# One scaling and one reciprocal for both halves of the heads, in a fused attention and two-layer feed-forward kernel

## The chip, the cores and the metric

The kernel runs on one core of a Trainium2 chip. The engines are TensorE (PE, matrix products; its weight loads are a row of their own, PEld), VectorE (DVE), ScalarE (ACT), GpSimdE (POOL) and SyncE (SP, which issues the transfers). The metric is the time of one execution on the device in microseconds.

## The reference

The reference computes attention of 8 heads over 4 batches (512 local positions with a window of 32 to each side, and 32 global ones), and two feed-forward layers behind it. What the change touches is the softmax of the local positions:

```
def sm(s):
    s = s - np.max(s, axis=-1, keepdims=True)
    e = np.exp(s)
    return e / (np.sum(e, axis=-1, keepdims=True) + 1e-09)
...
s_l = np.concatenate([s_lg, s_ll], axis=-1)      # scores of the local queries
a_l = sm(s_l)
out_l = np.matmul(a_l, np.concatenate([v_g, v_l], axis=2))
...
h = x @ w_in                                     # 2304 x 512 times 512 x 2048
g = np.where(h > 0.0, h, alpha * (np.exp(np.minimum(h, 0.0)) - 1.0))
y = g @ w_out
```

A gated layer (w_gate, w_val, a second w_out) follows.

## The kernel before, in words

**Attention units.** The local attention is cut into 16 units, u = 4 x batch + tile of 128 queries. A unit has two halves, par = 0 and 1: the even and the odd heads, four of each. It goes through these steps:

- `a_S` on TensorE: scores s, one tile of 4 x 128 columns in PSUM per half (L229 puts in the mask, L235 the products).
- `a_E`: VectorE finds the maxima of each half (L254) and multiplies them by −0.125 (L255) into one small tile mx; ScalarE then takes the exponentials, four instructions per half (L257), each with its column of mx as bias. Only the first eight units do it so; later units have another form (L248, L250), which returns ahead of these lines.
- `a_T`: TensorE transposes (L263, tile ptp), ScalarE copies out of PSUM (L265, tile ET).
- `a_PV` on TensorE: product with the values (L276), whose last column is the sum of the exponentials, into one tile o per half.
- `a_N` on VectorE, in all 16 units: add 1e-9 to the sums (L289), reciprocal (L290), multiply (L291) into the result x.

**Blocks.** The four units of a batch make the 512 tokens of one block of the first feed-forward layer. x is transposed (`a_X`, L299 to L301) into xT. A block has 16 hidden blocks j of 128 columns: `mm1` makes h(j) on TensorE (12 matmuls, L132); ScalarE (L121, L122) and VectorE (L123) form the activation; ScalarE rounds it (L139) and VectorE forms the rest by a subtraction (L140), which together are g(j); `mm2` multiplies g(j) by the second matrix into y (12 matmuls, L146, in two parts of six). The second matmul of each three needs the rest, and so L140. TensorE does h(j+1) ahead of y(j).

**Weight tasks.** The weights come as 64-bit numbers and are decoded on the chip. There are 16 tasks for the first layer, numbered 0 to 15: a load of 1 MB (L75), absolute values on ScalarE (L83, tile dx), four steps on bits on VectorE (L90, L91, L92, L93), a rounding cast on ScalarE (L96) and a subtraction on VectorE (L99) into a tile wA. The tiles raw and dx have few buffers, so L93 of one task frees the buffer for the load of a later one.

**Order.** Units 0 to 3 and tasks 0 to 2 stand in an order written by hand for VectorE and ScalarE (`tc.manual_schedule`, L411 on). TensorE's order is written by hand for the whole kernel. From the first block on, a scheduler of the language sets the order on VectorE, ScalarE and the queue of transfers; each engine then runs its instructions in the order in which they stand. Units 4 to 7 run inside block 0 (`att_slot`): for hidden blocks 4i to 4i+3, unit 4+i has its scores at the first, its transpositions between the two parts of y in the second, and its product with the values in the third. So unit 6 belongs to hidden blocks 8 to 11, and its transpositions stand in the middle of y(8).

Of the kernel before, what the change touches and what calls it, by code (L numbers as in the profile page):

```python
# [13 lines left out]
ALU = mybir.AluOpType  # L14
# [7 lines left out]
P = 128  # L22
# [4 lines left out]
SCALE = 0.125  # L27
# [15 lines left out]
def fused_kernel(ctx: ExitStack, tc: tile.TileContext, kq, vl, gkq, gv, w_in, w_out, w_gate, w_val, w_o2, rms_g, consts, out):  # L43
    nc = tc.nc
# [141 lines left out]
    with ExitStack() as ls:  # L186
# [52 lines left out]
        def a_E(u):  # L239
            ss = s_t.pop(u)  # L240
            mx = small.tile([P, 2, 4], F32, tag="st", name="mx")
            e = [ap_.tile([P, 4, P], F32, tag=f"E{par}", name="E") for par in range(2)]
            if u >= 8:
                T = u % 4
                mk_u = mask32[:, 0 if T == 0 else (2 if T == 3 else 1), :]
                for par in range(2):
                    for pr in range(4):
                        nc.vector.tensor_tensor_reduce(out=e[par][:, pr, :], in0=ss[par][:, pr, :], in1=mk_u, scale=-SCALE, scalar=3.0e38,  # L248
                                                       op0=ALU.add, op1=ALU.min, accum_out=mx[:, par, pr:pr + 1])
                        nc.scalar.activation(e[par][:, pr, :], e[par][:, pr, :], AF.Exp, bias=mx[:, par, pr:pr + 1], scale=-1.0)  # L250
                e_t[u] = e
                return
            for par in range(2):
                nc.vector.tensor_reduce(out=mx[:, par, :], in_=ss[par], axis=AX.X, op=ALU.max)  # L254
                nc.vector.tensor_scalar(out=mx[:, par, :], in0=mx[:, par, :], scalar1=-SCALE, scalar2=None, op0=ALU.mult)  # L255
                for pr in range(4):
                    nc.scalar.activation(e[par][:, pr, :], ss[par][:, pr, :], AF.Exp, bias=mx[:, par, pr:pr + 1], scale=SCALE)  # L257
            e_t[u] = e
# [21 lines left out]
        def a_N(u):  # L280
            b, T = u // 4, u % 4
            if T == 0:
                x_t[b] = moe.tile([P, 4, 512], F32, tag="x32", name="x")
            x = x_t[b][:, T, :].rearrange("p (a e d) -> p e a d", a=4, e=2)
            os_ = o_t.pop(u)
            st = small.tile([P, 2, 4, 2], F32, tag="st", name="st")
            for par in range(2):
                o = os_[par]
                nc.vector.tensor_scalar(out=st[:, par, :, 0:1], in0=o[:, :, 64:65], scalar1=1e-9, scalar2=None, op0=ALU.add)  # L289
                nc.vector.reciprocal(st[:, par, :, 1:2], st[:, par, :, 0:1])  # L290
                nc.vector.tensor_tensor(out=x[:, par], in0=o[:, :, 0:64], in1=st[:, par, :, 1:2].to_broadcast([P, 4, 64]), op=ALU.mult)  # L291

        def a_X(b, cs, xT, pools):

# [11 lines left out]
        def att_slot(b, j, part):  # L306

            u, jj = 4 * (b + 1) + j // 4, j % 4
            if jj == 0 and part == 0:
                a_S(u, ATT2)  # L310
                a_E(u)
                load_kq(u + 1)
            if jj == 1 and part == 1:
                a_T(u, 0, aps, "att")
                a_T(u, 1, aps, "att")
            if jj == 2 and part == 0:
                a_PV(u, ATT2)
                a_N(u)
                load_v(u + 1)
# [91 lines left out]
        with tc.manual_schedule(engines={mybir.EngineType.DVE, mybir.EngineType.Activation}):  # L411
# [11 lines left out]
            a_S(0, ATT2)  # L423
            w1_bits(0)
            a_E(0)
            a_S(1, HB)
            a_T(0, 0, yps, "y0")
            a_T(0, 1, yps, "y1")
            w1_hi(0)
            a_E(1)  # L430
            a_PV(0, Y2)
            w1_lo(0)
            a_N(0)
            w1_abs(1)
            a_S(2, ATT2)
# [3 lines left out]
            w1_bits(1)  # L439
            a_PV(1, Y2)  # L440
            a_N(1)
            a_S(3, HB)
            a_T(2, 0, yps, "y0")
# [651 lines left out]
```

## Time and profile before

| what | us |
|---|---|
| median of 3 runs (lowest, highest) | 898.16 (897.08, 898.88) |
| the profiled execution, its own time | 896.49 |
| its span in the trace | 894.4 |
| TensorE busy | 862.2 (96%) |
| VectorE busy | 593.3 (66%) |
| ScalarE busy | 477.8 (53%) |

The profile is of one execution. Its span is what the trace covers; its own time is 2.1 us more. Busy shares are over the whole span, in which the first 160 us, with the attention units, differ from the rest.

### The profile page before, as it was taken

Reading aid. Unit: us, or ns where it says so; the run is one execution under the profiler, and the core shown is the slowest. Engines: PE = TensorE matmul, PEld = TensorE weight load, DVE = VectorE, ACT = ScalarE, POOL = GpSimd, SP = SyncE. Lnnn points to the kernel's source line nnn. Section 1 sums busy time; section 2 is a strip of 40 time slices with the busy share of each in tenths; the row PEclk is TensorE's granted clock in tenths of the full one; section 3 lists DMA queues with packets and bytes.
Section 4 is the critical chain, followed back from the end, with each engine's and each line's share of the span. In section 5 each row is a group of like instructions: output and inputs, shape, how many; then the busy total and the mean of one; then the engine's idle time right before and its main releaser. Section 6 shows DMA issues by size and latency. Waiting matters only on the chain.

```text
span 894.4 us, 16208 instructions
## 1 busy us (share of the span) xinstructions
PE 862.2 (96%) x6588; PEld 736.3 (82%) x6588; DVE 593.3 (66%) x1079; ACT 477.8 (53%) x863; POOL 19.2 (2%) x22
## 2 busy tenths in 40 slices
PE   4779999999999999999999999999999999999997
PEld 3567877888888888677888899997999998899985
DVE  4899988787677763543489566884365776365642
ACT  4677665555565454433556646664455665355531
POOL 0000000000000000000110101000100000000000
PEclk9999999999999999999999999999999999999999
DMA  9785375976678642441405532233222242133201
GB/s 359 301 307 194 121 263 178 294 275 189 227 259 287 219 168 112 172 153 60 168 1 208 181 95 95 95 119 117 83 95 95 95 131 70 60 118 119 93 25 36
DMA packets 60370, 139.46 MB, mean 156 GB/s; under 512 B 4872, under 2 KB 30728, under 8 KB 57736
## 3 DMA queue, kind: packets, MB, share of 16 engines
q1 hardware_dynamic: 60296, 138.43, 44.8%
q8 instruction: 52, 0.85, 0.4%
q14 instruction: 22, 0.18, 0.1%
HBM read 115.35 MB, written 23.07 MB: 155 GB/s over the span
## 4 chain that ended last, share of the span: by engine, by line
PE 78%; DVE 10%; DMA 5%; ACT 4%; issue 2%; SPq 1%; POOL 0%; ACTq 0%
PE A L751 15%; PE y L146 15%; PE h L132 15%; PE o L757 15%; PE Q L751 11%; DMA kq<-in_kq 2%; DVE dx L93 1%; DVE dx L92 1%; PE s L235 1%; PE ptp L263 1%; PE o L276 1%; PE hg L687 1%; DMA raw<-in_moe_w_out 1%; DVE wA L99 1%; DVE dx L90 1%
## 5 line engine op out<-in xcount | busy, mean ns | idle before, releaser
L146 PE MATMUL y<-g,wA 128*128 128x512 f32 x768 | 198.0, 401 | 4.8 <-DVE g L140 4.1
L132 PE MATMUL h<-xT,wA 128*128 128x512 f32 x768 | 186.6, 392 | 1.8 <-DVE xT L301 1.8
L146 PEld LDWEIGHTS y<-g,wA 128*128 128x128 f32 x768 | 140.3, 189 | 40.5 <-DVE g L140 6.1
L132 PEld LDWEIGHTS h<-xT,wA 128*128 128x128 f32 x768 | 143.6, 188 | 32.7 <-DVE xT L301 2.4
L751 PE MATMUL A<-xc,wS 128*128 128x384 f32 (+1 forms) x864 | 156.0, 329 | 1.1 <-ACT t L958 0.6
L751 PEld LDWEIGHTS A<-xc,wS 128*128 128x128 f32 x864 | 145.0, 188 | 5.9 <-ACT t L958 0.9
L757 PE MATMUL o<-wB,p 128*128 128x512 f32 x612 | 147.4, 393 | 0.7 <-DVE p L762 0.3
L757 PEld LDWEIGHTS o<-wB,p 128*128 128x128 f32 x612 | 113.7, 188 | 24.6 <-DVE p L762 2.5
L751 PE MATMUL Q<-xc,wS 128*128 128x384 f32 (+1 forms) x648 | 115.3, 326 | 0.0
L751 PEld LDWEIGHTS Q<-xc,wS 128*128 128x128 f32 x648 | 107.8, 188 | 0.0
L607 DVE TENSOR_TENSOR wS<-wraw,wS 128x1024 fp32r<-128x1024 f32 x63 | 78.5, 1246 | 35.7 <-ACT wS L606 35.6
L766 DVE TENSOR_TENSOR t<-t,Q 128x384 f32<-128x384 f32 (+1 forms) x108 | 55.9, 528 | 36.6 <-PE Q L751 24.0
L606 ACT CAST wS<-wraw 128x1024 fp32r<-128x1024 f32 x63 | 65.9, 1050 | 18.5 <-PE Q L751 11.4
L121 ACT ACTIVATE e<-h 128x512 f32<-128x512 f32 x48 | 28.9, 602 | 78.8 <-PE h L132 78.7
L139 ACT CAST g<-e 128x512 fp32r<-128x512 f32 x64 | 39.7, 621 | 48.8 <-DVE e L123 32.2
L123 DVE SCALAR_TENSOR_TENSOR e<-e,h 128x512 f32<-128x512 f32 x48 | 32.6, 679 | 34.8 <-ACT e L122 34.8
L140 DVE TENSOR_TENSOR g<-e,g 128x512 fp32r<-128x512 f32 x64 | 43.9, 686 | 10.1 <-ACT g L139 9.7
L762 DVE TENSOR_TENSOR p<-p,p 128x384 fp32r<-128x384 f32 x36 | 20.0, 557 | 43.1 <-ACT p L761 43.1
L83 ACT ACTIVATE dx<-raw 128x1024 f32<-128x1024 f32 x34 | 38.9, 1148 | 10.5 <-DMA raw<-in_moe_w_out 3.5
L92 DVE SCALAR_TENSOR_TENSOR dx<-raw,dx 128x1024 int32<-128x1024 int32 x34 | 42.1, 1245 | 0.8
L93 DVE SCALAR_TENSOR_TENSOR dx<-raw,dx 128x1024 int32<-128x1024 int32 x34 | 41.4, 1220 | 0.3
L761 ACT CAST p<-p 128x384 fp32r<-128x384 f32 x36 | 18.4, 514 | 41.6 <-PE o L757 41.5
(176 smaller groups left out, 872.1 us busy)
## 6 DMA issues: line engine op xcount, KB each, us to landing
wraw<-wS SPq DMA_DIRECT2D x63, 512.0 KB, 3.2
raw<-in_moe_w_out SPq DMA_DIRECT2D x14, 1024.0 KB, 7.6
raw<-in_moe_w_in SPq DMA_DIRECT2D x8, 1024.0 KB, 7.2
raw<-in_moe_w_gate SPq DMA_DIRECT2D x6, 1024.0 KB, 5.6
raw<-in_moe_w_val SPq DMA_DIRECT2D x6, 1024.0 KB, 6.4
wS<-raw SPq DMA_DIRECT2D x48, 128.0 KB, 2.3
gvr<-in_gv SPq DMA_DIRECT2D x8, 640.0 KB, 4.1
wS<-dx SPq DMA_DIRECT2D x36, 128.0 KB, 2.1
```

The source lines that it names most:

```text
L83: ins = nc.scalar.activation(x, f(words(raw)[:, :, 1]), AF.Abs)
L92: nc.vector.scalar_tensor_tensor(out=i32(x), in0=word[:, :, 1], scalar=-0x40000000, in1=i32(x), op0=ALU.bitwise_and, op1=ALU.bitwise_or)
L93: nc.vector.scalar_tensor_tensor(out=i32(x), in0=word[:, :, 0], scalar=29, in1=i32(x), op0=ALU.logical_shift_right, op1=ALU.bitwise_or)
L132: nc.tensor.matmul(h[:, :n], W1[c, G][:, ws, o:o + P], xT[c][:, xs, :n], start=(k == 0), stop=(k == 11))
L139: nc.scalar.copy(g[:, 0, :n], e[:, :n])
L140: nc.vector.tensor_tensor(out=g[:, 1, :n], in0=e[:, :n], in1=f(g[:, 0, :n]), op=ALU.subtract)
L146: nc.tensor.matmul(ys[dc][:, :n], W2[j][:, ws, dc * P:(dc + 1) * P], g[:, gs, :n], start=(j == 0 and k == 0), stop=(j == 15 and k == 2))
L606: nc.scalar.copy(t[:, :, 0, :], raw)
L607: nc.vector.tensor_tensor(out=t[:, :, 1, :], in0=raw, in1=f(t[:, :, 0, :]), op=ALU.subtract)
L751: nc.tensor.matmul(ps[:, :n], w[:, 2 * (q % 4) + c, ws, :], x[:, c, xs, :n], start=(first and c == 0 and z == 0), stop=(c == 1 and z == 2) ...
L757: nc.tensor.matmul(o, p[:, pp, t * P:(t + 1) * P], Wo[j][:, ww, :], start=(first and z == 0), stop=(last and z == 2))
L766: nc.vector.tensor_tensor(out=t, in0=t, in1=ps, op=ALU.add)
```

## The change

In `a_E` of the first eight units the scaling of the maxima is one operation on 8 columns behind both reduces, where it was one on 4 columns behind each. In `a_N` of all units the two additions come first, then one reciprocal of 8 columns, then the two multiplications. There are 24 VectorE instructions fewer (8 scalings, 16 reciprocals). The lines of the exponentials, the copies and the multiplications become L258, L266 and L292.

```
             for par in range(2):
                 nc.vector.tensor_reduce(out=mx[:, par, :], in_=ss[par], axis=AX.X, op=ALU.max)
-                nc.vector.tensor_scalar(out=mx[:, par, :], in0=mx[:, par, :], scalar1=-SCALE, scalar2=None, op0=ALU.mult)
+            nc.vector.tensor_scalar(out=mx, in0=mx, scalar1=-SCALE, scalar2=None, op0=ALU.mult)
+            for par in range(2):
                 for pr in range(4):
                     nc.scalar.activation(e[par][:, pr, :], ss[par][:, pr, :], AF.Exp, bias=mx[:, par, pr:pr + 1], scale=SCALE)
...
             for par in range(2):
-                o = os_[par]
-                nc.vector.tensor_scalar(out=st[:, par, :, 0:1], in0=o[:, :, 64:65], scalar1=1e-9, scalar2=None, op0=ALU.add)
-                nc.vector.reciprocal(st[:, par, :, 1:2], st[:, par, :, 0:1])
-                nc.vector.tensor_tensor(out=x[:, par], in0=o[:, :, 0:64], in1=st[:, par, :, 1:2].to_broadcast([P, 4, 64]), op=ALU.mult)
+                nc.vector.tensor_scalar(out=st[:, par, :, 0:1], in0=os_[par][:, :, 64:65], scalar1=1e-9, scalar2=None, op0=ALU.add)
+            nc.vector.reciprocal(st[:, :, :, 1:2], st[:, :, :, 0:1])
+            for par in range(2):
+                nc.vector.tensor_tensor(out=x[:, par], in0=os_[par][:, :, 0:64], in1=st[:, par, :, 1:2].to_broadcast([P, 4, 64]), op=ALU.mult)
```

TensorE's order is the same as before. The scheduler's order on VectorE and ScalarE changes between the first subtraction L140 and the end of block 0. Three places follow, before and with the change; numbers of tiles differ between the two programs.

ScalarE around the exponentials of unit 6, before. dx_1373 and wA_1379 are of weight task 12, g_1242 of hidden block 8, e_1340 of block 9, E_1288 and E_1289 the exponentials of unit 6:

```order
L83 ACTIVATE dx_1457<-raw_1180 128x1024
L139 CAST g_1242<-e_1238 128x512
L257 ACTIVATE E_1288<-s_1245,mx_1287 128x128 x4
L257 ACTIVATE E_1289<-s_1246,mx_1287 128x128 x4
L121 ACTIVATE e_1340<-h_1327 128x512
L122 ACTIVATE e_1340<-e_1340 128x512
L265 COPY ET_1358<-ptp_1353 128x512
L265 COPY ET_1365<-ptp_1360 128x512
L96 CAST wA_1379<-dx_1373 128x2x512
L139 CAST g_1344<-e_1340 128x512
```

The exponentials stand right behind the rounding of block 8, ahead of block 9's activation and of task 12's cast.

The same place with the change. wA_1366 is of task 12, dx_1484 of task 14, g_1230 of block 8, e_1327 of block 9, E_1276 and E_1277 are unit 6:

```order
L83 ACTIVATE dx_1443<-raw_1168 128x1024
L139 CAST g_1230<-e_1226 128x512
L121 ACTIVATE e_1327<-h_1314 128x512
L122 ACTIVATE e_1327<-e_1327 128x512
L96 CAST wA_1366<-dx_1360 128x2x512
L258 ACTIVATE E_1276<-s_1233,mx_1275 128x128 x4
L258 ACTIVATE E_1277<-s_1234,mx_1275 128x128 x4
L139 CAST g_1331<-e_1327 128x512
L266 COPY ET_1345<-ptp_1340 128x512
L83 ACTIVATE dx_1484<-raw_1211 128x1024
L266 COPY ET_1352<-ptp_1347 128x512
```

Block 9's activation and task 12's cast moved ahead of the exponentials, and task 14's absolute values between the two copies behind them.

VectorE from the subtraction of block 8 (g_1242) on, before; mx_1287 are unit 6's maxima:

```order
L255 TENSOR_SCALAR mx_1287<-mx_1287 128x4
L140 TENSOR_TENSOR g_1242<-e_1238,g_1242 128x512
L255 TENSOR_SCALAR mx_1287<-mx_1287 128x4
L91 TENSOR_SCALAR dx_1373<-dx_1373 128x1024
L91 TENSOR_SCALAR dx_1457<-dx_1457 128x1024
L92 SCALAR_TENSOR_TENSOR dx_1373<-raw_1094,dx_1373 128x1024
L92 SCALAR_TENSOR_TENSOR dx_1457<-raw_1180,dx_1457 128x1024
L93 SCALAR_TENSOR_TENSOR dx_1373<-raw_1094,dx_1373 128x1024
L123 SCALAR_TENSOR_TENSOR e_1340<-e_1340,h_1327 128x512
```

The scalings stand on both sides of the subtraction.

With the change, from the subtraction of block 8 (g_1230) on; dx_1360 is task 12, dx_1443 task 13:

```order
L140 TENSOR_TENSOR g_1230<-e_1226,g_1230 128x512
L93 SCALAR_TENSOR_TENSOR dx_1360<-raw_1083,dx_1360 128x1024
L255 TENSOR_SCALAR mx_1275<-mx_1275 128x8
L91 TENSOR_SCALAR dx_1443<-dx_1443 128x1024
L123 SCALAR_TENSOR_TENSOR e_1327<-e_1327,h_1314 128x512
L92 SCALAR_TENSOR_TENSOR dx_1443<-raw_1168,dx_1443 128x1024
L99 TENSOR_TENSOR wA_1366<-dx_1360,wA_1366 128x2x512
L93 SCALAR_TENSOR_TENSOR dx_1443<-raw_1168,dx_1443 128x1024
L140 TENSOR_TENSOR g_1331<-e_1327,g_1331 128x512
```

The one scaling of unit 6 stands behind task 12's L93, which stands behind the subtraction; block 9's subtraction (g_1331) has one L91 and one L92 fewer ahead of it.

VectorE between the subtractions of blocks 9 (g_1344) and 10 (g_1399), before; st_1436 and o_1402 belong to unit 6, dx_1498 to task 14:

```order
L140 TENSOR_TENSOR g_1344<-e_1340,g_1344 128x512
L99 TENSOR_TENSOR wA_1463<-dx_1457,wA_1463 128x2x512
L289 TENSOR_SCALAR st_1436<-o_1402 128x4
L289 TENSOR_SCALAR st_1436<-o_1403 128x4
L123 SCALAR_TENSOR_TENSOR e_1395<-e_1395,h_1382 128x512
L290 RECIPROCAL st_1436<-st_1436 128x4 x2
L90 TENSOR_SCALAR dx_1498<-dx_1498 128x1024
L291 TENSOR_TENSOR x_861<-o_1402,st_1436 128x4x64
L291 TENSOR_TENSOR x_861<-o_1403,st_1436 128x4x64
L140 TENSOR_TENSOR g_1399<-e_1395,g_1399 128x512
```

With the change, up to the subtraction of block 10 (g_1386); ahead of these rows stand L90 and L91 of task 14 (dx_1484) behind block 9's subtraction, and dx_1583 is task 15:

```order
L99 TENSOR_TENSOR wA_1449<-dx_1443,wA_1449 128x2x512
L92 SCALAR_TENSOR_TENSOR dx_1484<-raw_1211,dx_1484 128x1024
L93 SCALAR_TENSOR_TENSOR dx_1484<-raw_1211,dx_1484 128x1024
L90 TENSOR_SCALAR dx_1583<-dx_1583 128x1024
L289 TENSOR_SCALAR st_1423<-o_1389 128x4
L123 SCALAR_TENSOR_TENSOR e_1382<-e_1382,h_1369 128x512
L289 TENSOR_SCALAR st_1423<-o_1390 128x4
L91 TENSOR_SCALAR dx_1583<-dx_1583 128x1024
L290 RECIPROCAL st_1423<-st_1423 128x8
L99 TENSOR_TENSOR wA_1490<-dx_1484,wA_1490 128x2x512
L92 SCALAR_TENSOR_TENSOR dx_1583<-raw_1312,dx_1583 128x1024
L140 TENSOR_TENSOR g_1386<-e_1382,g_1386 128x512
```

Task 14 whole, and half of task 15, moved ahead of block 10's subtraction. In the queue of transfers one pair changes places: the values of unit 7 now stand behind the first weights of the gated layer.

## Rows read from the trace of the kernel before

**Rows 1.** Busy us of each engine by stretch; then clock, transfers' share, GB/s.

```profile
60.00:80.00 20.00, 18.70 (x147) 14.74 (x147) 20.00 (x32) 12.46 (x18) 0.00 (x0) 1.00 0.77 286
160.00:300.00 140.00, 140.00 (x1293) 114.25 (x1292) 106.88 (x236) 74.79 (x138) 0.00 (x0) 1.00 0.76 255
```

**Rows 2.** Timeline of VectorE, unit 0's maxima: start, duration, engine, instruction.

```profile
14.35 0.68 DVE L254 TENSOR_REDUCE mx<-s 128x4 f32<-128x512 f32 x1
15.07 0.17 DVE L255 TENSOR_SCALAR mx<-mx 128x4 f32<-128x4 f32 x1
15.15 0.69 DVE L254 TENSOR_REDUCE mx<-s 128x4 f32<-128x512 f32 x1
```

**Rows 3.** Timeline of VectorE, a stretch without gaps, for steps between starts.

```profile
120.77 1.22 DVE L93 SCALAR_TENSOR_TENSOR dx<-raw,dx 128x1024 int32<-128x1024 int32 x1
121.90 0.69 DVE L91 TENSOR_SCALAR dx<-dx 128x1024 int32<-128x1024 int32 x1
122.50 0.68 DVE L123 SCALAR_TENSOR_TENSOR e<-e,h 128x512 f32<-128x512 f32 x1
123.10 1.22 DVE L92 SCALAR_TENSOR_TENSOR dx<-raw,dx 128x1024 int32<-128x1024 int32 x1
124.24 1.22 DVE L99 TENSOR_TENSOR wA<-dx,wA 128x1024 fp32r<-128x1024 f32 x1
```

**Rows 4.** Timeline of VectorE, unit 0's normalization, first half and start of the second.

```profile
20.78 0.15 DVE L289 TENSOR_SCALAR st<-o 128x4 f32<-128x4 f32 x1
20.97 0.18 DVE L290 RECIPROCAL st<-st 128x4 f32<-128x4 f32 x1
21.18 0.42 DVE L291 TENSOR_TENSOR x<-o,st 128x256 f32<-128x256 f32 x1
21.52 0.15 DVE L289 TENSOR_SCALAR st<-o 128x4 f32<-128x4 f32 x1
```

**Rows 5.** Timeline of three engines at the start; idle time before, and its releaser, in brackets.

```profile
19.64 1.23 DVE L99 TENSOR_TENSOR wA<-dx,wA 128x1024 fp32r<-128x1024 f32 x1 [2.01 <-ACT wA L96]
...
30.28 2.17 ACT L257 ACTIVATE E<-s,mx 128x128 f32<-128x128 f32 x8 [1.62 <-DVE mx L255]
...
33.92 1.15 PE L276 MATMUL o<-v,ET 128*32 128x65 f32 x64 [1.04 <-ACT ET L265]
...
36.29 1.64 PE L299 MATMUL xtp<-ident,x 128*128 128x128 f32 x13 [0.74 <-DVE x L291]
```

**Rows 6.** Timeline of VectorE and TensorE in hidden blocks 1 and 2.

```profile
55.89 0.69 DVE L90 TENSOR_SCALAR dx<-dx 128x1024 f32<-128x1024 f32 x1 [0.64 <-ACT dx L83]
...
66.49 2.79 PE L146 MATMUL y<-g,wA 128*128 128x512 f32 x11 [1.30 <-DVE g L140]
```

**Rows 7.** Timeline of VectorE, ScalarE and TensorE around hidden block 8 and unit 6.

```profile
104.51 0.69 DVE L140 TENSOR_TENSOR g<-e,g 128x512 fp32r<-128x512 f32 x1
...
104.70 2.17 ACT L257 ACTIVATE E<-s,mx 128x128 f32<-128x128 f32 x8 [0.39 <-DVE mx L255]
...
109.91 1.05 ACT L96 CAST wA<-dx 128x1024 fp32r<-128x1024 f32 x1 [0.93 <-DVE dx L93]
...
105.37 1.53 PE L146 MATMUL y<-g,wA 128*128 128x512 f32 x6
...
107.54 1.62 PE L146 MATMUL y<-g,wA 128*128 128x512 f32 x6
```

**Rows 8.** Timeline of the queue of transfers, ScalarE and TensorE, tasks 14 and block 10.

```profile
109.95 2.09 SPq L75 DMA_DIRECT2D raw<-in_moe_w_out  x2
...
114.87 1.12 ACT L83 ACTIVATE dx<-raw 128x1024 f32<-128x1024 f32 x1 [1.02 <-DMA raw<-in_moe_w_out]
...
118.73 2.88 PE L146 MATMUL y<-g,wA 128*128 128x512 f32 x12
```

**Rows 9.** TensorE behind its longest wait: busy by stretch with clock, and the timeline.

```profile
48.00:54.00 6.00, 3.69 (x14) 3.10 (x15) 5.96 (x10) 5.54 (x14) 0.00 (x0) 0.72 1.01 401
...
50.31 2.50 PE L146 MATMUL y<-g,wA 128*128 128x512 f32 x5 [2.57 <-DVE g L140]
```

## The prediction

> **What bounds the kernel now.** I first read busy time by stretch of time. From 160 us on TensorE is busy in all of the time, so whatever it loses before then moves the end by as much [rows 1]. Between 60 and 80 us VectorE is busy without a gap and TensorE is not: there VectorE's order of work decides when TensorE gets its next operand [rows 1]. That stretch holds the scheduled units 4 to 7, where the weight tasks, the hidden blocks and the attention units share VectorE. So a saving on VectorE can be worth something, and a change in its order can cost as much. The profiled execution took 896.49 us, 1.67 below the median of the three runs shown, 898.16; I make the sum against the profiled execution and add the result to the median.
>
> **The single operations.** In the first units each half took 0.72 us from the reduce to its dependent scaling and 0.08 us from there to the next reduce, 1.60 us for both halves [rows 2]. The trace has no two adjacent reduces followed by one scaling, nor an operation on eight elements. Independent operations of about 0.68 us start 0.60 us after each other [rows 3], so I take 0.60 + 0.72 + 0.08 = 1.40: 0.20 us less per unit on VectorE. Its bound is 0 below (a wider operation as dear as two) and 0.24 above (with the removed scaling its own 0.17 and the step behind it, at most). But the first half's exponentials now wait for the second half's reduce, 0.60 us more. The normalization took 0.19 + 0.21 + 0.34 per half, 1.48 us [rows 4]; merged it is 0.07 + 0.19 + 0.21 + 0.34 + 0.34 = 1.15, or 0.33 less, once both halves of the output are there. I take four elements more in an operation as free: the 0.17 us of 4 elements against 0.68 us of 512 leaves about 1 ns an element [rows 2].
>
> **The start (units 0 to 3, order written by hand).** The 0.60 us goes down ScalarE's queue, through the exponentials of unit 0 to the cast that VectorE's subtraction at 19.64 waited 2.01 us for [rows 5]; that subtraction moves to 20.24. Behind it the savings work it off: unit 0's normalization saves 0.33, unit 2's scaling 0.20, unit 1's normalization 0.33, so VectorE reaches unit 3's reduces 0.26 to 0.35 us sooner. The 0.60 us wait of unit 3's own exponentials takes that back: they start at about 30.5 instead of 30.28 [rows 5]. The product with the values follows them, from 33.92 to 34.15, ends at 35.30 instead of 35.07, and only then can the merged reciprocal of unit 3 start: 35.35 + 0.19 + 0.21 + 0.34 + 0.43 is 36.5, where the transpositions went on at 36.29 [rows 5]. **Start: +0.3 us**, bounded by −0.3 (all the wait hidden) and +0.6 (none).
>
> **VectorE's order up to hidden block 8.** The scheduler changed it: the difference of the two orders, counted from the subtraction of block 0 to that of block 8 (L140), is three scalings and two reciprocals fewer, but one L91 and one L92 more ahead of it. By the steps between starts [rows 3], 0.60 + 1.14, that is 1.74 less 5 x 0.07 to 0.08: +1.4 us. Against it stands an idle 0.64 us, in which VectorE waited for task 5's absolute values [rows 6]; they now come ahead of two copies on ScalarE, and VectorE reaches them later, so that gap closes. **Net +0.8 us**, between +0.4 and +1.4. With the start, block 8's subtraction moves from 104.51 to about 105.6 [rows 7].
>
> **The wait at unit 6.** Before, ScalarE ran unit 6's eight exponentials from 104.70, ahead of everything of block 9, and TensorE went through the transpositions without a wait into the second half of y(8) at 107.54 [rows 7]. Now block 8's subtraction is followed on VectorE by task 12's L93 and only then by the scaling, and on ScalarE by task 12's cast, which needs that L93, ahead of the exponentials. From the subtraction's start: 0.60, then L93 1.22 [rows 3], the cast 1.05, the exponentials 2.17, and about 0.15 for the last transposition [rows 7]. That is 5.2 us, so y(8)'s second half starts at 105.6 + 5.2 = 110.8. It was 3.03 behind the subtraction. **+3.2 us in all at this point**, of which 2.1 is the new wait. Queued behind the exponentials are block 9's cast and the copies that unit 6's product with the values needs; TensorE comes to them late as well.
>
> The Trainium skill, "PSUM — Partial Sum Buffer", Engine vs sequencer instructions, states that ScalarE's, VectorE's and GpSimdE's queues are strict first in, first out, which speaks against this change: by it the exponentials cannot pass the cast. By it the sum below stands; without it the exponentials could start with their maxima, the 2.1 us would go and 900.9 us would come out. The trace agrees where it can: VectorE stood 2.01 us behind a cast with other work queued [rows 5].
>
> **The wait at hidden block 10.** Between the subtractions of blocks 9 and 10 VectorE had one L90 and one L99 of the weight tasks before; now two L90, two L91, two L92, one L93 and two L99 stand there. Block 9's subtraction comes at 105.6 + 0.60 + 1.13 + 0.07 + 0.60 + 0.60 + 1.14 + 1.13 + 1.13 = 112.0. Then VectorE wants task 14, whose load took 4.9 us from issue at 109.95 to 114.87 [rows 8]; its buffer is now free at 105.6 + 1.8, so it lands near 112.4 and ScalarE has it done at 113.5. Task 13's cast stands behind that and a copy of half its size: 113.5 + 0.55 + 1.05 = 115.1. From there VectorE does L99, L92, L93, L90, two L289, L123, L91, the reciprocal, L99, L92: 4 x 1.14 + 1.26 + 3 x 0.60 + 3 x 0.07, near 7.9 us (1.26 is an L92 whose successor needs it, 0.12 more, as from a reduce to its scaling [rows 2]), and block 10's subtraction starts at 123.0, done at 123.8. TensorE reaches y(10) by 110.8 + (118.73 − 107.54) = 122.0 at the latest [rows 7, 8], and its second matmul needs that operand at 122.2. It waits 1.6 us or a little more. Before, that matmul ran at 118.96; now at 123.85. **+4.9 us in all at this point.** What hid the subtraction before was that it stood ahead of tasks 14 and 15; 0 to 2.4 us of wait are the bounds, by an earlier and a later landing of task 14.
>
> **The sum.** 0.3 + 0.8 + 2.1 + 1.7 = 4.9. After block 10 VectorE has idle time again and TensorE sets the pace, so nothing gives it back [rows 1]. The other edits cost nothing that ends last: in units 8 to 15 only reciprocals merge, beside a TensorE that never waits; if that cover were gone they would save 0.08 us each. In profiled time 896.49 + 4.9 = 901.4; on the median **898.16 + 4.9, about 903.0 us**.
>
> **Rivals.**
> *The saving comes through (faster).* Four units x (0.20 + 0.33), four x 0.15 for two operations fewer, eight x 0.08: 3.3 us, time 894.9. For it: VectorE full from 60 to 80 us [rows 1]. It decides if L93 and the cast of task 12 finish before TensorE needs unit 6, which takes VectorE 2 us ahead of my sums. Chance 0.08.
> *One wait only.* Unit 6 waits, block 10 does not, because task 14 lands earlier or TensorE comes later: +3.2 us, 901.4. Chance 0.15.
> *The clock falls as well.* After a wait of 2.57 us TensorE's five matmuls took 2.50 us, against six in 1.53 later, with a granted clock of 0.72 over that stretch, that is between its two levels of 1.2 and 2.4 GHz; after 1.30 us it did not fall (11 matmuls in 2.79) [rows 6, 7, 9]. The new waits, about 1.4 us with half-busy transpositions behind it and 1.6 to 2.1 us, lie between these. A fall costs about 1.2 us each: 904.2 to 905.5. Chance 0.25.
> *No change.* The lateness is absorbed: VectorE's order is as good as the old one, and my sums of it are too long by the 3 us or so that the two waits need. Against it speaks that the cast stands ahead of the exponentials whatever the times are. Within 0.2%, near 898.2. Chance 0.12.
>
> **How the numbers follow.** My forecast, both waits at an unchanged clock, has 0.40 and its own range 901.9 to 904.0. The range for all, 899.0 to 906.0, leaves out the faster case and most of no change. Beyond 0.2%, 1.8 us, a measurement of this kernel tells a time from no change. Slower: 0.40 + 0.25 + 0.15 = 0.80; same 0.12; faster 0.08.
>
> **What would show it.** The profile after should have a wait of transpositions for exponentials between 107 and 111 us, a wait of y for L140 near 122 us, full busy time behind 160 us, the reciprocal once per unit, and the transpositions of the first block going on at 36.6 instead of 36.29. I am wrong if unit 6's exponentials start by 106, if block 8's subtraction stands before 105 us, or if waits of over 1 us appear or go in the stretch 145 to 155 us, which I take as unchanged.

## The result, and the profile after

The changed kernel took 903.51 us (median of 6 runs, 902.13 to 905.26) against 898.45 us for the kernel before (6 runs, 897.08 to 899.21): the ratio is 1.0063, with a 95% interval of 1.0052 to 1.0073. In a second set of runs it was 1.0071 (1.0055 to 1.0087). The change makes the kernel slower by 5 to 6 us; 903.0 was predicted.

The profiled execution of the changed kernel took 903.48 us, close to its median. That of the kernel before took 896.49 us, 1.96 us under the median of these six runs, so that the two traces differ by 7.0 us where the medians differ by 5.06. I read places from the traces and sizes from the medians.

The busy time by stretch answers to [rows 1]; columns are PE, PEld, DVE, ACT, POOL, granted clock, transfers' share, GB/s:

```profile
60.00:80.00 20.00, 19.10 (x208) 14.93 (x207) 20.00 (x28) 11.73 (x15) 0.00 (x0) 1.00 0.74 263
160.00:300.00 140.00, 140.00 (x1252) 114.13 (x1233) 105.17 (x240) 77.33 (x146) 0.00 (x0) 1.00 0.75 252
```

VectorE still has no gap between 60 and 80 us, and TensorE still has none from 160 to 300 us: what is lost before then stays lost. The merged operations on VectorE's timeline (units 0 and 1, maxima, then unit 0's normalization) answer to [rows 2, 4]:

```profile
14.10 1.28 DVE L254 TENSOR_REDUCE mx<-s 128x4 f32<-128x512 f32 x2
15.41 0.17 DVE L255 TENSOR_SCALAR mx<-mx 128x8 f32<-128x8 f32 x1
15.49 1.28 DVE L254 TENSOR_REDUCE mx<-s 128x4 f32<-128x512 f32 x2
...
21.13 0.23 DVE L289 TENSOR_SCALAR st<-o 128x4 f32<-128x4 f32 x2
21.39 0.20 DVE L290 RECIPROCAL st<-st 128x8 f32<-128x8 f32 x1
21.63 0.76 DVE L292 TENSOR_TENSOR x<-o,st 128x256 f32<-128x256 f32 x2
```

A unit's maxima take 15.49 − 14.10 = 1.39 us (before 1.60, predicted 1.40). Eight elements cost what four did, 0.17. So each single step came out as worked out, to 0.03 us, and the saving on VectorE's own time is real. The start, from the timelines of VectorE and TensorE, answers to [rows 5]:

```profile
19.99 1.23 DVE L99 TENSOR_TENSOR wA<-dx,wA 128x1024 fp32r<-128x1024 f32 x1 [3.01 <-ACT wA L96]
...
32.57 1.09 PE L277 MATMUL o<-v,ET 128*32 128x65 f32 x30 [2.40 <-issue]
...
33.59 1.97 PE L264 MATMUL ptp<-ident,E 128*128 128x128 f32 x8
...
38.22 1.64 PE L300 MATMUL xtp<-ident,x 128*128 128x128 f32 x13 [0.83 <-DVE x L292]
```

The transpositions go on at 38.22, 1.93 us later than before and not 0.3. The subtraction waits 3.01 us for the cast, where it waited 2.01. Two things on TensorE add to it: a gap of 2.40 us inside unit 2's product with the values (1.40 before, also put down to "issue": the profile shows nothing that was waited for), and a lower granted clock behind it. The same product and unit 3's transpositions in the kernel before:

```profile
31.20 0.66 PE L276 MATMUL o<-v,ET 128*32 128x65 f32 x30 [1.40 <-issue]
31.79 1.09 PE L263 MATMUL ptp<-ident,E 128*128 128x128 f32 x8
```

The clock by stretch, in the changed kernel:

```profile
30.00:34.00 4.00, 1.59 (x38) 1.26 (x33) 0.91 (x5) 3.11 (x9) 0.00 (x0) 0.77 1.04 429
34.00:38.00 4.00, 3.30 (x75) 2.47 (x73) 3.12 (x9) 2.33 (x3) 0.00 (x0) 0.81 0.99 372
```

The same two stretches of the kernel before:

```profile
30.00:34.00 4.00, 1.75 (x42) 1.42 (x45) 2.95 (x10) 3.72 (x11) 0.00 (x0) 1.00 1.04 430
34.00:38.00 4.00, 3.19 (x80) 2.62 (x80) 2.80 (x9) 2.85 (x5) 0.00 (x0) 1.00 1.02 378
```

The clock is 0.77 and 0.81 where it was 1.00, so for part of the time TensorE ran at the lower of its two levels. Hidden block 8 and unit 6, from the timelines of VectorE, ScalarE and TensorE, answer to [rows 7]:

```profile
107.56 0.69 DVE L140 TENSOR_TENSOR g<-e,g 128x512 fp32r<-128x512 f32 x1
108.16 1.22 DVE L93 SCALAR_TENSOR_TENSOR dx<-raw,dx 128x1024 int32<-128x1024 int32 x1
109.29 0.17 DVE L255 TENSOR_SCALAR mx<-mx 128x8 f32<-128x8 f32 x1
...
109.41 1.05 ACT L96 CAST wA<-dx 128x1024 fp32r<-128x1024 f32 x1
110.37 2.17 ACT L258 ACTIVATE E<-s,mx 128x128 f32<-128x128 f32 x8
...
111.56 0.66 PE L264 MATMUL ptp<-ident,E 128*128 128x128 f32 x4 [1.83 <-ACT E L258]
112.59 0.66 PE L264 MATMUL ptp<-ident,E 128*128 128x128 f32 x4 [0.38 <-ACT E L258]
113.00 1.64 PE L146 MATMUL y<-g,wA 128*128 128x512 f32 x6
```

The chain is the predicted one, link by link: subtraction, L93, cast, exponentials, transpositions. From the subtraction to the second half of y(8) it takes 113.00 − 107.56 = 5.44 us, predicted 5.2, before 3.03. The scaling itself was done at 109.46; the exponentials then stood behind the cast for 0.9 us although they lacked nothing. Hidden block 10, the same three engines:

```profile
115.49 0.70 DVE L90 TENSOR_SCALAR dx<-dx 128x1024 f32<-128x1024 f32 x1 [0.83 <-ACT dx L83]
...
124.87 0.69 DVE L140 TENSOR_TENSOR g<-e,g 128x512 fp32r<-128x512 f32 x1
...
123.90 0.39 PE L146 MATMUL y<-g,wA 128*128 128x512 f32 x1
125.61 2.79 PE L146 MATMUL y<-g,wA 128*128 128x512 f32 x11 [1.32 <-DVE g L140]
```

y(10)'s second matmul waits 1.32 us for the subtraction, at an unchanged clock (11 matmuls in 2.79). Before, it ran 6.65 us earlier. All waits of TensorE from 60 to 300 us, longest last in a row:

```profile
PE y L146 <- DVE g L140: 2.9, 3, 1.3
PE ptp L264 <- ACT E L258: 2.6, 3, 1.8
PE h L132 <- DVE xT L302: 0.5, 1, 0.5
```

In the kernel before these three were 1.3, 0.4 and 0.5 us. So the two predicted waits are there, and no third of over 1 us.

### The profile page after: what moved, and what is told of

The parts are those of the page before. It is cut to its first block, busy times and chain, and to the rows that moved or that the text cites. A ratio compares the mean times of both kernels' runs of the same rounds, so it can differ in the third digit from the quotient of the medians.

```text
span 901.6 us, 16174 instructions
## 1 busy us (share of the span) xinstructions
PE 864.9 (96%) x6588; PEld 736.5 (82%) x6588; DVE 591.2 (66%) x1055; ACT 478.8 (53%) x863; POOL 19.2 (2%) x22
## 4 chain that ended last, share of the span: by engine, by line
PE 82%; DVE 7%; DMA 5%; ACT 3%; issue 2%; SPq 0%; POOL 0%; ACTq 0%
PE y L146 17%; PE h L132 16%; PE A L752 15%; PE o L758 14%; PE Q L752 11%; DMA kq<-in_kq 2%; PE s L235 2%; PE o L277 1%; PE ptp L264 1%; DVE dx L92 1%; DMA raw<-in_moe_w_in 1%; PE hg L688 1%; DMA wraw<-wS 1%; PE go L860 1%; DVE dx L93 1%
## 5 line engine op out<-in xcount | busy, mean ns | idle before, releaser
L140 DVE TENSOR_TENSOR g<-e,g 128x512 fp32r<-128x512 f32 x64 | 44.0, 687 | 10.4 <-ACT g L139 10.0
L92 DVE SCALAR_TENSOR_TENSOR dx<-raw,dx 128x1024 int32<-128x1024 int32 x34 | 42.3, 1246 | 0.8
L93 DVE SCALAR_TENSOR_TENSOR dx<-raw,dx 128x1024 int32<-128x1024 int32 x34 | 41.6, 1223 | 0.3
```

What stands on the lines that cost most here:

```text
L92: nc.vector.scalar_tensor_tensor(out=i32(x), in0=word[:, :, 1], scalar=-0x40000000, in1=i32(x), op0=ALU.bitwise_and, op1=ALU.bitwise_or)
L93: nc.vector.scalar_tensor_tensor(out=i32(x), in0=word[:, :, 0], scalar=29, in1=i32(x), op0=ALU.logical_shift_right, op1=ALU.bitwise_or)
L140: nc.vector.tensor_tensor(out=g[:, 1, :n], in0=e[:, :n], in1=f(g[:, 0, :n]), op=ALU.subtract)
```

## The experiments

In block 0 an order can be imposed on VectorE and ScalarE instruction by instruction, with the work itself unchanged. That separates the two things that the change did at once: it merged operations, and it made the scheduler choose another order. To follow a loss or a gain through a run I took from each trace the starts of TensorE's product h and subtracted those of the kernel before. Each column is one start, named by its time before; each row is one profiled execution, in us:

| kernel | 39.22 | 55.37 | 83.21 | 108.99 | 121.45 | 149.45 | 175.45 | 480.27 |
|---|---|---|---|---|---|---|---|---|
| changed kernel | +1.9 | +2.3 | +2.9 | +5.5 | +6.8 | +6.1 | +6.1 | +5.8 |
| the same, again | +1.5 | +3.3 | +3.3 | +6.0 | +7.5 | +6.8 | +6.8 | +6.4 |
| start_only | +0.2 | +0.3 | +0.2 | +0.2 | +0.2 | −0.2 | −0.2 | −0.4 |
| merged_old_order | +1.7 | +3.5 | +3.6 | +3.9 | +3.6 | +4.0 | +4.0 | +3.7 |
| split_new_order | −0.2 | +0.2 | +0.8 | +3.6 | +5.2 | +4.7 | +4.7 | +4.4 |
| unit6_early | +2.1 | +2.5 | +3.1 | +3.7 | +10.7 | +10.1 | +10.0 | +9.8 |
| block10_early | +1.3 | +3.2 | +3.4 | +6.0 | +5.6 | +5.0 | +5.0 | +4.6 |
| both_early | +2.4 | +2.8 | +3.1 | +3.8 | +3.5 | +3.5 | +5.0 | +4.6 |
| order_split | +0.6 | −2.5 | −4.4 | −4.4 | −4.7 | −3.1 | +4.2 | +3.9 |
| order_merged | +0.7 | −2.7 | −5.0 | −4.5 | −4.9 | −3.8 | +2.7 | +2.3 |
| order_split_2 | +0.6 | −2.5 | −4.5 | −4.5 | −4.9 | −1.3 | +0.7 | +0.8 |
| order_merged_2 | +0.2 | −3.3 | −5.5 | −5.1 | −5.5 | −4.5 | −0.8 | −1.1 |
| order_merged_3 | +2.2 | −1.2 | −3.5 | −3.1 | −3.4 | −1.9 | −0.5 | +4.1 |

Differences to before by the medians are given below as the ratio's, times the median of before in the same set of runs, with the 95% interval in brackets.

### Order or merging: three kernels

**start_only** merges in units 0 to 3 alone (the edit is against the changed kernel; the later units keep the two steps of before):

```diff
-            nc.vector.tensor_scalar(out=mx, in0=mx, scalar1=-SCALE, scalar2=None, op0=ALU.mult)
+            if u < 4:
+                nc.vector.tensor_scalar(out=mx, in0=mx, scalar1=-SCALE, scalar2=None, op0=ALU.mult)
...
-            nc.vector.reciprocal(st[:, :, :, 1:2], st[:, :, :, 0:1])
+            if u < 4:
+                nc.vector.reciprocal(st[:, :, :, 1:2], st[:, :, :, 0:1])
```

> Both operations are merged in units 0 to 3 alone, the ones in the order written by hand; all other units stay split, and the order of block 0 is that of the kernel before. Order theory (the time is lost in the scheduler's new order of block 0): +0.3 us, about 898.7. Rival (the waiting for both halves at the start is what costs; in the changed kernel's profile the first transpositions went on 1.9 us later than before): +1.9 us, about 900.4.

Measured: 897.86 against 897.40, ratio 1.0003 (0.9993 to 1.0013), +0.3 us (−0.6 to +1.2). Its transpositions went on at 36.49. As the order theory had it; +1.9 lies outside the interval. So the merging at the start does not by itself cost the 1.93 us that the changed kernel's profile shows there.

**merged_old_order** is the whole change with the order of before in block 0 (the diff is in the order alone: one list per engine, each instruction tied behind the one ahead of it in the list):

```diff
+        in_order(<VectorE's instructions of block 0 as before, second scaling and second reciprocal only>)
+        in_order(<ScalarE's instructions of block 0 as before>)
```

> The whole change, but in block 0 VectorE and ScalarE run their instructions in the order of the kernel before (the merged scaling and reciprocal stand where the second of each pair stood). Order theory: nearly all of the loss goes, the start's +0.3 and the few tenths saved by the merging remain: 898.0 to 898.8. Rival (the merging itself costs, since each merged step waits for both halves): the loss stays, about 903.

Measured: 899.09 against 897.40, ratio 1.0015 (1.0001 to 1.0028), +1.3 us (0.1 to 2.5). The two waits are gone, and 903 is excluded; but it is 1 us dearer than I gave it. Its row in the table shows where: the start, and +1.8 between 39 and 55 us. There unit 4's one scaling stands behind an L99, since the second of the pair had stood there; its exponentials started at 53.16 (50.73 before, and 1.7 of the difference are the start), the transpositions waited 0.96 us for them, and the six matmuls behind ran in 2.91 us instead of 1.64, with a granted clock of 0.50 from 54 to 58 us. The changed kernel's order has the scaling behind the same L99, so this cost is not peculiar to the order of before: the second profile of the changed kernel (after_again, below), in the scheduler's order, loses 1.8 us there as well. First merged_old_order, then after_again:

```profile
54.35 2.14 PE L290 MATMUL ptp<-ident,E 128*128 128x128 f32 x8 [0.96 <-ACT E L284]
56.15 2.91 PE L167 MATMUL y<-g,wA 128*128 128x512 f32 x6
...
54.19 2.15 PE L264 MATMUL ptp<-ident,E 128*128 128x128 f32 x8 [0.79 <-ACT E L258]
55.98 2.91 PE L146 MATMUL y<-g,wA 128*128 128x512 f32 x6
```

In the first profile of the changed kernel the five matmuls ahead of the transpositions were slower (2.20 us, against 1.43 in merged_old_order), the wait was 0.20 and the loss 0.4. What this place costs differs between executions.

**split_new_order** merges nothing and takes the changed kernel's order:

```diff
-                nc.vector.tensor_scalar(out=mx, in0=mx, scalar1=-SCALE, ...)   # one for both halves
+                <one for each half, side by side>; reciprocals likewise
+        in_order(<VectorE's and ScalarE's instructions of block 0 as in the changed kernel>)
```

> Nothing is merged: the operations are those of the kernel before, but in block 0 VectorE and ScalarE run in the order of the changed kernel (the pairs of scalings and reciprocals side by side where the merged one stands). Order theory: +4.6 us, about 903. Rival (the merging itself costs): no change, about 898.5.

Measured: 902.29 against 897.40, ratio 1.0048 (1.0033 to 1.0063), +4.3 us (3.0 to 5.7). The order alone brings both waits, without a single merged operation. From TensorE's timeline:

```profile
109.67 0.66 PE L290 MATMUL ptp<-ident,E 128*128 128x128 f32 x4 [1.82 <-ACT E L279]
...
124.05 2.79 PE L167 MATMUL y<-g,wA 128*128 128x512 f32 x11 [1.65 <-DVE g L161]
```

1.82 and 1.65 us, against 1.83 and 1.32 in the changed kernel. In its trace ScalarE's queue and the queue of transfers have the changed kernel's order throughout. So 4.3 of the 5 to 6 us come with the scheduler's order alone. The whole merging in the order of before costs 1.3 us (0.1 to 2.5); in neither kernel of that order is it a saving that the medians show.

### Putting the order back in pieces: three kernels

**unit6_early**, on VectorE and on ScalarE:

```diff
 L140 of block 8
+L255 of unit 6
 L93 of task 12
-L255 of unit 6
...
+L258 of unit 6, x8
 L121, L122 of block 9
 L96 of task 12
-L258 of unit 6, x8
```

> The changed kernel with one edit of its order: unit 6's scaling goes ahead of task 12's L93, and its eight exponentials ahead of block 9's activation and task 12's cast, as before the change. The wait at unit 6 (1.8 us) should go. Theory (VectorE's order still lets block 10's subtraction start at 124.9 us, so TensorE only waits there longer, 3 us and more where it was 1.3): 902.9 to 903.5. Rival (the two waits simply add up): 1.8 to 2.1 us of the loss go, about 901.5.

Measured: 906.67 against 897.40, ratio 1.0097 (1.0079 to 1.0115), +8.7 us, 3 us more than the changed kernel. The rival is refuted, and my theory, which had no extra loss, missed as well. The wait of 1.83 us at unit 6 did go. From VectorE's, ScalarE's and TensorE's timelines:

```profile
111.97 0.69 DVE L144 SCALAR_TENSOR_TENSOR e<-e,h 128x512 f32<-128x512 f32 x1 [1.72 <-ACT e L143]
...
114.85 1.31 DVE L93 SCALAR_TENSOR_TENSOR dx<-raw,dx 128x1024 int32<-128x1024 int32 x1
...
121.42 1.13 ACT L83 ACTIVATE dx<-raw 128x1024 f32<-128x1024 f32 x1 [3.73 <-DMA raw<-in_moe_w_out]
...
125.20 0.50 PE L167 MATMUL y<-g,wA 128*128 128x512 f32 x1 [2.06 <-ACT g L160]
128.08 4.23 PE L167 MATMUL y<-g,wA 128*128 128x512 f32 x11 [2.38 <-DVE g L161]
```

Block 9's activation, now behind the exponentials, kept VectorE waiting for 1.72 us; task 13's L93 behind it started at 114.85 instead of 112.83; that L93 frees the buffer for task 15's load, so task 15's absolute values came at 121.42 instead of 118.91; and on ScalarE block 10's activation stood behind them. y(10) then waited twice, 2.06 and 2.38 us, and its 11 matmuls took 4.23 us, with a granted clock of 0.68 from 128 to 133 us, where they take 2.79 at 1.00. The wait had moved to the end of a chain through a transfer and grown.

**block10_early** takes the order of before from block 9's subtraction to the end of block 0, on VectorE and on ScalarE. The part on VectorE up to block 10's subtraction:

```diff
 L140 of block 9
-L90, L91 of task 14
 L99 of task 13
-L92, L93 of task 14, L90 of task 15
 L289 x2, L123 of block 10, L290 of unit 6
-L91 of task 15, L99 of task 14, L92 of task 15
+L90 of task 14, L292 x2
 L140 of block 10
```

> The changed kernel, but from hidden block 9's subtraction on VectorE and ScalarE have the order of the kernel before, so that block 10's subtraction stands ahead of tasks 14 and 15. Unit 6's wait is left as it is. Theory of two waits (each costs what it shows): the wait of y(10) for L140 goes, that of unit 6's transpositions stays: 1.3 to 1.7 us of the loss go, so +3.2 to +3.8 us against before. Rival (what is lost at unit 6 only reappears further down, as it did when unit 6 alone was put back): no gain, +5 us.

Measured: 902.06 against 897.71, ratio 1.0049 (1.0032 to 1.0066), +4.4 us (2.9 to 5.9). The wait at block 10 is gone from the trace. Between the starts at 108.99 and 121.45 its row gains some 0.3 us where the two profiles of the changed kernel lose 1.3 and 1.5; at 149.45 it lies 1.1 and 1.8 us ahead of them, to either side of the 1.3 to 1.7 expected. By the medians the interval holds both theories; by the trace it is the theory of two waits.

**both_early** is the two edits together:

```diff
+<the edit of unit6_early>
+<the edit of block10_early>
```

> Both edits of the order together: unit 6's scaling and exponentials ahead of task 12, and block 10's subtraction ahead of tasks 14 and 15. Theory of two waits: what is left is the start (+0.3 us) and VectorE's order up to block 8 (+0.8 us): about +1.1 us against before, and no wait of over 1 us behind 60 us. Rival (block 9's activation, now behind the exponentials, holds the next block back): +3 us or more.

Measured: 902.01 against 897.71, ratio 1.0051 (1.0032 to 1.0071), +4.6 us (2.9 to 6.4). A miss. Between 60 and 300 us no wait of TensorE is over 0.7 us, as expected, and from 55 to 149 us only 0.7 us are lost. But its start was 2.4 us late, and 1.4 us went between 149 and 175 us, in the second block, where ScalarE waited 3.07 us for a transfer ahead of a cast. I had summed the waits of the first block as though nothing stood behind it. The scheduler also ordered the second block anew: in the queue of transfers a load of kq, which stands behind that weight load in the kernel before, went ahead of it, and the weight load was issued at 161.53 us (157.29 before), 4.2 us later, while TensorE was 2.9 us late. Whether the new place or the late start of the block makes the wait, no run separates.

### An order of my own: five kernels

The dearest wait of the kernel before is that of y(0) for hidden block 0's subtraction: 2.57 us, with a clock of 0.72 around it [rows 9]. Steps of task 3, which y(0) does not need, stand ahead of that subtraction. I laid out block 0's two queues by when TensorE wants each result, once for all merged (order_merged) and once for pairs kept apart (order_split); the two orders are of one kind, and differ in more than the pairs. The first rows of VectorE's, as order_merged has them:

```diff
 L93 of task 2
-L123 of block 0, L93 of task 3
-L254 x2 of unit 4
+L254 of unit 4, L123 of block 0
 L99 of task 2
+L254 of unit 4
 L140 of block 0
+L255 of unit 4, L91, L92, L93 of task 3
...
```

> The operations of the kernel before, nothing merged, in an order of my own on VectorE and ScalarE in block 0, which puts each step by when TensorE wants it: the subtraction of hidden block 0 ahead of task 3, weight tasks as late as their hidden blocks allow. If VectorE's order is what sets the time of block 0, the wait of 2.57 us at y(0) and the slow matmuls behind it go and no wait of over 1 us appears: 4 to 6 us less than before. If the order is not what sets it (VectorE's work is too much in any order): no change or slower.

> The changed kernel, all merged, with an order of the same kind in block 0. If the merging is harmless once the order suits it: the same gain against before as with nothing merged, within 1 us, 4 to 6 us less. If merging by itself costs time in block 0: at least 2 us more than the version with nothing merged.

Measured: 901.40 and 899.98 against 897.71, ratios 1.0045 (1.0027 to 1.0062) and 1.0034 (1.0017 to 1.0051). Slower, both. Yet block 0 does what was expected: the table has them 4.4 and 5.0 us ahead at 83.21 and still 3 to 4 us ahead at 149.45. All of it, and more, goes in one place of the second block. From order_merged's ScalarE and TensorE timelines:

```profile
165.04 1.12 ACT L83 ACTIVATE dx<-raw 128x1024 f32<-128x1024 f32 x1 [6.16 <-DMA raw<-in_moe_w_val]
...
166.72 5.88 PE L167 MATMUL y<-g,wA 128*128 128x512 f32 x12 [3.37 <-ACT g L160]
```

A weight task of the gated layer waits 6.16 us for its transfer, the cast of the hidden block stands behind it, TensorE stands 3.37 us, and then takes 5.88 us for 12 matmuls that took 3.00 (granted clock 0.66 from 165 to 175 us). The transfers themselves have no slack there, even in the kernel before (last columns: granted clock, transfers' share, GB/s):

```profile
160.00:170.00 10.00, 10.00 (x108) 8.20 (x107) 9.90 (x16) 5.68 (x10) 0.00 (x0) 1.00 1.02 326
```

TensorE comes 4 us early to a stretch in which the transfers are busy all the time. That they set its pace is argued and not shown: as in both_early, the kq load stands ahead of this weight load in the own orders. The next two kernels move that task behind the cast and the activation that it held up:

```diff
+L139 of block 17, L122 of block 18 -> ahead of L83 of that task   (ScalarE; blocks counted through)
+L140 of block 17, L123 of block 18 -> ahead of its L90, L140 of block 18 ahead of its L92   (VectorE)
```

> As the own order with nothing merged, and one more edit: in the second block the absolute values of one weight task of the gated layer, which waited 6 us for their transfer at 165 us with the cast of the next hidden block queued behind them, go behind that cast. If that queue is what took back the gain of block 0 (3 us ahead before it, 4 us behind after it, a clock fall included): 3 to 5 us less than before. If the transfer itself is what the block waits for: the wait reappears a hidden block later and nothing is gained.

> The same edit in the own order with all merged. If merging is harmless once the order suits it: 3 to 5 us less than before and within 1 us of the version with nothing merged. If merging costs by itself: less gain than that by 1 us or more.

Measured: 897.02 and 896.00 against 898.21, ratios 0.9985 (0.9973 to 0.9997) and 0.9976 (0.9964 to 0.9989): −1.3 us (−2.4 to −0.3) and −2.2 us (−3.2 to −1.0). Both are faster than the kernel before, by less than the 3 to 5 us expected. So the merged operations do not keep a kernel from being faster than before, under an order that suits them; the 1 us between the two kernels does not measure the merging, since their orders differ. What remains of the loss in order_merged_2 is a wait of y for its subtraction, with a slow stretch behind it:

```profile
170.39 4.38 PE L167 MATMUL y<-g,wA 128*128 128x512 f32 x11 [1.86 <-DVE g L161]
```

The last kernel moves the task further back:

```diff
-L140 of block 17, L123 of block 18 -> ahead of its L90, L140 of block 18 ahead of its L92
+L139 of block 18 -> ahead of its L83; L140 of block 18 -> ahead of its L90; L123 of block 19 -> ahead of its L93
```

> The own order with all merged; the late weight task of the second block now goes behind the cast and the subtraction of that hidden block too, and the next block's activation ahead of its last step. If the queue behind the late transfer is all that is left: the wait of 1.9 us at 170 us and the slow matmuls behind it go, 4 to 5 us less than before. If TensorE, now early, finds the next transfer late as well: the wait moves again, and 2 us less than before remain.

Measured: 901.72 against 897.84, ratio 1.0043 (1.0027 to 1.0059), +3.9 us. Worse than without. VectorE's timeline has the reason for the first part of it:

```profile
170.89 0.76 DVE L322 TENSOR_TENSOR x<-o,st 128x256 f32<-128x256 f32 x2 [4.42 <-DMA yT<-yev]
171.56 0.68 DVE L161 TENSOR_TENSOR g<-e,g 128x512 fp32r<-128x512 f32 x1
```

With the weight task out of the way, VectorE came to unit 8's multiplication, whose result shares a buffer with an output still on its way to memory, and stood 4.42 us with the subtraction behind it. At 200 us a further wait, of 2.37 us for a cast, took 4.9 us with the slow matmuls behind it. The wait moved, as the second branch of the expectation had it, but the 2 us that were to remain became a loss of 3.9: a miss.

**after_again** is the changed kernel without an edit.

> The changed kernel once more, timed and profiled on the same chip as the others. Theory: +5 us against before again (+4.0 to +6.0). For the start: if the 1.9 us by which the first transpositions went on later in the changed kernel's profile belong to the change, they come at 38.0 to 38.4 again; if they are what one profile differs from another, the time lies between 36.3 and 37.5 now.

Measured: 903.35 against 897.84, ratio 1.0071 (1.0055 to 1.0087), +6.4 us (4.9 to 7.8). Its transpositions went on at 37.80, between the two cases that I had named, with the clock at 0.80 and 0.77 from 30 to 38 us.

## Why the prediction held, and where its terms were off

- **The single operations.** Right: 1.39 us per unit against 1.40. The Trainium skill, "Perfetto Trace Analysis", Optimizing Scalar/DVE Operations, says that grouping into larger operations can improve throughput where the engine is saturated. By that page the merge could pay between 60 and 80 us, where VectorE has no gap. The trace agrees on the engine's own time and not on the kernel's: each operation saved is a step of 0.07 to 0.08 us there, and what decided was the order in which the rest then stood.
- **The start, +0.3.** Too small in the profiles. start_only's median gives +0.3 (−0.6 to +1.2), but the first product h starts at 40.65 us in the mean of the ten profiles with a merged start (39.38 to 41.64) and at 39.45 in the four without (38.98 to 39.80): 1.2 us apart, each profile scattering by about 1. The working followed the dependences through VectorE and ScalarE and left out what TensorE does there: in the changed kernel's profile the second part of unit 2's product starts at 32.57, behind the gap of 2.40 us, instead of 31.20, and takes 0.43 us longer, which together puts unit 3's transpositions 1.80 us later (33.59 against 31.79). That gap is 1.40 to 2.40 us in the fourteen profiles, and what makes it no run shows. The lower clock does not go with the lateness by itself: start_only had 0.57 from 30 to 34 us and was 0.2 us late, order_merged had 1.00 and was 0.7 us late. How much of the 1.2 us belongs to the change and how much to the execution that was profiled stays open.
- **VectorE's order up to block 8, +0.8.** 107.56 − 104.51 = 3.05, less the start's 1.93: +1.1, inside its bounds of 0.4 to 1.4. In split_new_order, with an earlier start, it is 105.67 − 104.51 + 0.24 = +1.4.
- **The wait at unit 6, +2.1.** 5.44 − 3.03 = +2.4, through the named chain. That the order makes it was shown by split_new_order, and that the place of the scaling and the exponentials makes it by unit6_early, where it vanished.
- **The wait at block 10, +1.7.** 6.65 − 5.46 = +1.2 here, with waits of 1.32, 1.49 and 1.65 us in three profiles of this order. Block 10's subtraction came 1.9 us later than worked out and TensorE 2.1 us, so their distance nearly held.
- **"Nothing gives it back."** Nearly: of 6.8 us at 121 us, 6.1 are left at 149 us.
- **The clock rival.** It fell out: the granted clock is 1.00 at both new waits. In unit6_early, where y(10) waited 2.06 and 2.38 us in a row, 11 matmuls did take 4.23 us, and in order_merged_2 they took 4.38 us behind a single wait of 1.86 us. The working could not tell these cases from the waits of 1.82 and 1.83 us that left the clock at 1.00, so that the rival stayed away is luck as far as the working goes.
- **The saving comes through**, the rival on the other side, needed TensorE not to reach unit 6 before its exponentials were done. It needed another order for that, and under one (order_merged_2) the merged kernel does end 2.2 us below the kernel before. What that order gains in block 0, 5 us, is lost in large part in the second block, behind late transfers.

Added up from the runs: the order alone +4.3 (my terms 0.8 + 2.1 + 1.7 = 4.6), the merging in the order of before +1.3 (my term 0.3), together 5.6 where 5.1 to 6.4 was measured. The mechanism held; that the sum of 4.9 came within 0.2 us of the medians' 5.06 is in part luck. In the two profiles, which lie 7.0 us apart, the terms are 1.9 + 1.1 + 2.4 + 1.2 = 6.6: the start too small in the working, block 10 too large. The working also had no term for unit 4, whose transpositions waited for the one scaling's exponentials (0.20 and 0.79 us in the two profiles of the changed kernel).

## What to carry to other kernels

Where a scheduler orders the queues, an edit that saves a tenth of a microsecond can cost five through the order that comes out: read the new order first, and look for what now stands between a result and the engine that waits for it. To tell the edit from the order, run the old work in the new order and the new work in the old one. Before putting one wait right, follow what stands behind it in each queue to the next transfer: taking away a wait of 1.8 us here made the kernel 3 us slower, and 5 us gained in one block were lost behind a late transfer in the next.

## What the runs showed of the hardware beyond that

The start of the kernel is not the same from run to run: in kernels whose start has the same instructions the first product h came between 39.38 and 41.64 us, and the granted clock of TensorE between 34 and 38 us was 1.00 in some profiles and 0.50 in that of both_early. The price of a wait of TensorE is not proportional to its length either. A wait of 1.83 us at 111 us left the clock at 1.00; one of 1.86 us, in the second block of order_merged_2, was followed by 11 matmuls in 4.38 us instead of 2.79. And a TensorE that is busy in all of a stretch does not say that it alone bounds it: the transfers stood at a share of 1.02 from 160 to 170 us of the kernel before, where TensorE was busy in all of the 10 us, and kernels that came there earlier then waited behind them (order_split, order_merged).
